# Reordering the first tiles' second state product, one weight conversion and the last stores in a fused attention and gated-MLP kernel

## The chip, the cores and the metric

The kernel runs on one core of a Trainium2 chip. The metric is the device time of one execution in microseconds (us). The core has five engines with their own instruction streams: TensorE (PE in the profile, with weight loads as PEld), VectorE (DVE), ScalarE (ACT), GpSimd (POOL) and SyncE (SP), which here only issues transfers. Each engine runs its stream in order; the engines wait for each other through semaphores. An instruction that has to wait therefore holds up everything behind it on its engine.

## The reference

An attention block with B = 8 batches, H = 8 heads, S = 512 tokens, Ns = 32 states and head size 64, then an MLP over 4352 rows (8 x (512 + 32)) with model width 512 and inner width 2048:

```python
scores = scale * np.matmul(x, state.transpose(0, 1, 3, 2))
a = softmax(scores)                     # over the 32 states
xread = np.matmul(a, state)
scores2 = scale * np.matmul(state, x.transpose(0, 1, 3, 2))
sread = np.matmul(softmax(scores2), x)  # over the 512 tokens
y = concatenate([xread, sread], axis=2) -> rows of 512
h = y @ w_in
out = (h * np.cos(h)) @ w_out
```

The function `softmax` stands here for the max, exp, sum and division that the reference writes out. The inputs x and state are float32. The two weights are float64, 8 MB each.

## The kernel before, in words

The attention output of the tokens is never formed. For a batch, "products" (L433) multiplies the batch's states by 512 columns of w_in, giving the *state product*, and evicts it to a tile `sw` with "products_kept" (ScalarE) or "products_taken" (VectorE), L438 to L447. The hidden value of a tile is then the normalised attention matrix aT times sw. There are four such products (nt = 0 to 3) for each batch; "second state product" means nt = 1 of the first batch. The fifth tile of the first batch is the first whose hidden value needs it.

A *tile* is 128 inner columns for the 512 tokens of one batch: 16 tiles a batch, 128 in all, and 16 more for the 256 state rows. One tile takes these steps:

- `hidden` (L466): TensorE forms h in one of two PSUM buffers.
- `gate` (L475, ScalarE): adds a large constant, which rounds.
- `gate2` (L478, VectorE): the rest after rounding.
- `gate3` (L483 and L484, ScalarE): absolute value and sine, which gives the cosine.
- `gate4` (L490, VectorE): h times cosine, into a slot of `g_all`. It also frees the PSUM buffer of h.
- `output` (L609), three to four tiles later: TensorE multiplies g with w_out. The tokens' output goes through sums and differences of blocks ("Pair", L500 to L547; L496 on GpSimd or VectorE). The state rows' output (`state_output`, L648) is summed in the two PSUM tiles `acc[MAIN]`.

The weights arrive as float64 in 18 loads of up to 1 MB (and two more late ones) through SyncE's queue into three raw buffers in turn. A load is *converted* to float32 by steps in `convert_part` (L217): "1" and "2" on ScalarE (L224, L227), "a", "b" and "c" on VectorE (L231, L233, L236), and "d", an integer addition, on GpSimd (L241). Step "f" fetches a later load. The step "a" limits small values from below with a maximum: this is the "limit" of the change's name. The table `conv_at` (L804) says at which step's end a load is converted; normally "1" and "2" run in that step, and "abcdf" in the next step, after gate2. Load 5 (the sixth) was an exception: all of it stood at the end of step 1, on VectorE between gate4 of the second tile and gate2 of the third.

Nothing is reordered by a scheduler: the loop at L824 writes one step for each tile, and the order of its calls is the order on every engine. `todo` holds the attention parts that `plan` (L733) puts into each step. They include, at steps 1 to 4, the first batch's state reads: "turn", "reads" (L406), "keep" (L416), "keep2" (L422) and "keep3" (L427). After the reads, `load_x(1)` (L104) fetches the second batch's image in eight transfers; its tokens are turned on TensorE at step 5 (L271). `warm` (L694) issues matmuls whose results are not used, only to keep TensorE busy; they write a PSUM tile that is begun afresh later.

At the end, the last three state tiles are put out after the loop, each with one matmul for the first half of the rows and one for the second. Then ScalarE evicts both halves (L660) and SyncE issues eight stores (L665).

The three lines that set the place of the second state product before the change were:

```python
        if step == 4:
            part(0, "products", 1, SIDE)
            part(0, "products_kept", 1, SIDE)
```

Of the kernel before, what the change touches and what calls it, by code (L numbers as in the profile page):

```python
# [9 lines left out]
F32 = mybir.dt.float32  # L10
# [3 lines left out]
ACTF = mybir.ActivationFunctionType  # L14
# [5 lines left out]
TWO_PI = 2.0 * math.pi  # L20
# [3 lines left out]
def kernel(  # L24
# [8 lines left out]
    nc = tc.nc  # L33

    B, H, S, D = x.shape
    Ns = state.shape[2]
    Dm, Dff = moe_w_in.shape
    P = 128
    NK = Dm // P
    NF = Dff // P  # L40
    NC = S // P
    T = S + Ns
    WC = 512
    scale = 1.0 / math.sqrt(D)
# [6 lines left out]
    osb = ctx.enter_context(tc.tile_pool(name="osb", bufs=2))  # L51
# [19 lines left out]
    w_out = consts.tile([P, 2, NF, HD], F32)  # L71
# [32 lines left out]
    def load_x(b):  # L104

        src = x[b].rearrange("h (c p) d -> p c h d", p=P)
        if b < 2:
            for h in range(H):
                nc.sync.dma_start(out=x_b[:, :, h], in_=src[:, :, h])
        else:  # L110
            for c in range(NC):
                nc.sync.dma_start(out=x_b[:, c], in_=src[:, c])
# [10 lines left out]
    def load_state(half, queues):  # L123
        b = slice(4 * half, 4 * half + 4)
        for k in range(NK):
# [11 lines left out]
    acc = [[ops.tile([P, S], F32, name=f"o{m}{ch}") for ch in range(2)]  # L137
           for m in range(2)]
# [41 lines left out]
    def fetch(n):  # L180
        nonlocal n_fetched
        while n_fetched < n:
            dst, src = loads[n_fetched]
            if f64:
                m, w = dst.shape[1:]

                at_, c0 = (n_fetched - 2) % 3, 0
                if n_fetched < 4:
                    at_, c0 = n_fetched // 2, n_fetched % 2 * 2 * m * w
                if n_fetched >= N_LOADS:  # L190
                    at_ = 3 + n_fetched - N_LOADS
                raw = raw_at[at_].bitcast(I32)[:, c0:c0 + 2 * m * w]
                raw = raw.rearrange("p (m f) -> p m f", m=m)
                nc.sync.dma_start(out=raw, in_=src.bitcast(I32))
                raws[n_fetched] = raw.rearrange("p m (f w) -> p m f w", w=2)
            else:
                nc.sync.dma_start(out=dst, in_=src)
            n_fetched += 1
# [6 lines left out]
    def convert(i, parts):  # L205

        for p in parts:  # L210
            if p == "f":
                if i not in (1, 2) and i + 3 < N_LOADS:
                    fetch(max(i + 4, 6))
            elif f64:
                convert_part(i, p)

    def convert_part(i, p):  # L217
        raw, dst = raws[i], loads[i][0]
        bits = dst.bitcast(I32)
        m, w = dst.shape[1:]  # L220
        c0 = m * w if i in (2, 3) else 0
        e = low[i % 2][:, c0:c0 + m * w].rearrange("p (m f) -> p m f", m=m)
        if p == "1":
            nc.scalar.activation(dst, raw.bitcast(F32)[:, :, :, 1],  # L224
                                 func=ACTF.Abs)
        elif p == "2":
            nc.scalar.activation(e, raw.bitcast(U32)[:, :, :, 0],  # L227
                                 func=ACTF.Copy, scale=2.0 ** -51, bias=2.0)
        elif p == "a":
            engine = nc.gpsimd if i == 1 else nc.vector  # L230
            engine.tensor_scalar(dst, dst, 2.0 ** -15, None, op0=ALU.max)  # L231
        elif p == "b":
            nc.vector.tensor_scalar(bits, bits, 3, None,  # L233
                                    op0=ALU.logical_shift_left)
        elif p == "c":
            nc.vector.scalar_tensor_tensor(out=bits, in0=raw[:, :, :, 1],  # L236
                                           scalar=-2 ** 31, in1=bits,
                                           op0=ALU.bitwise_and,
                                           op1=ALU.bitwise_xor)
        else:  # L240
            nc.gpsimd.tensor_tensor(bits, bits, e.bitcast(I32), op=ALU.add)  # L241
# [209 lines left out]
    def part(b, name, *args):  # L451

        if b not in attn:
            attn[b] = Attention(b)
        getattr(attn[b], name)(*args)
        if (name, args) == ("reads", (1,)) and b + 1 < B:
            if b > 0:
                attn[b + 1] = Attention(b + 1)
                attn[b + 1].load_tokens()
            load_x(b + 1)  # L460
# [5 lines left out]
    def hidden(t):  # L466
        t.hp = hps.tile([P, S], F32, name="h")[:, 0:t.n]
        for i in range(t.kn):
            nc.tensor.matmul(out=t.hp, lhsT=t.lhs(i), rhs=t.rhs(i),  # L469
                             start=(i == 0), stop=(i == t.kn - 1))  # L470

    def gate(t):

        t.q = msb.tile([P, S], F32, name="q")[:, 0:t.n]
        nc.scalar.activation(t.q, t.hp, func=ACTF.Copy, bias=MAGIC)  # L475

    def gate2(t):
        nc.vector.scalar_tensor_tensor(out=t.q, in0=t.q, scalar=MAGIC,  # L478
                                       in1=t.hp, op0=ALU.subtract,
                                       op1=ALU.subtract)  # L480
# [17 lines left out]
    MAIN, SIDE = 0, 1  # L498
# [90 lines left out]
    def free(t):  # L589
        g_free.append(t.slot)  # L590
# [54 lines left out]
                store(2 * pr.n + 1, 0, o)  # L645


    def state_output(t):  # L648
        n, pr = t.n_th, t.last_pair
        for i in range(2):  # L650
            nc.tensor.matmul(out=acc[MAIN][i],  # L651
                             lhsT=t.g[:, P * i:P * i + P],
                             rhs=w_out[:, :, t.f, :],
                             start=(n == 0), stop=(n == NF - 1))
        free(t)
        pr.more(2)
        if n == NF - 1:
            for i in range(2):
                ot = osb.tile([P, Dm], F32, name="ot")
                nc.scalar.activation(ot, acc[MAIN][i], func=ACTF.Copy,  # L660
                                     scale=TWO_PI)
                nb = P // Ns
                for m in range(nb):
                    r0 = (nb * i + m) * T + S
                    nc.sync.dma_start(out=out[r0:r0 + Ns, :],  # L665
                                      in_=ot[Ns * m:Ns * m + Ns, :])

    def tiles():
        pr = None
# [24 lines left out]
    def warm(n, to):  # L694

        for _ in range(n):
            nc.tensor.matmul(out=to, lhsT=zeros[:, 0:P], rhs=zeros, start=True,
                             stop=True)
# [34 lines left out]
    def plan(b):  # L733
# [70 lines left out]
    conv_at = {s: 4 + i for i, s in enumerate(  # L804
        (0, 1, 2, 3, 4, 5, 6, 7, 8, 10, 11, 12, 13, 14))}
# [18 lines left out]
    for step, t in enumerate(all_tiles):  # L824
        s = step % NF
        if s == 0 and t.b < B:
            steps = plan(t.b)
        todo = [p[s] if t.b < B else [] for p in steps]

        def go(n):  # L830
            for p in todo[n]:
                part(*p)

        last, conv = conv_at.get(step - 1, -1), conv_at.get(step, -1)
        if step == B * NF + (0 if f64 else 8):
            fetch(N_LOADS + 2)
        if step == 4:
            part(0, "products", 1, SIDE)
            part(0, "products_kept", 1, SIDE)
        if step != 1:  # L840
            hidden(t)
        if step == 0:
            hidden(all_tiles[1])
            warm(3, acc[MAIN][0])
            gate(t)
            gate2(t)
            convert(3, "bcdf")
            convert(4, "1a")
            go(0)
        else:  # L850
            go(0)
            if step == 5:
                states(1, acc[SIDE][1])
            gate(t)
            gate2(t)
            go(1)
            go(3)
            if step == 1:
                convert(4, "bcdf")
            elif last >= 0:  # L860
                convert(last, "abcdf")
            if conv >= 0 and not todo[1]:
                convert(conv, "1")
        gate3(t)
        if later:
            later.pop(0)()
        gate4(t)
        if conv >= 0 and todo[1] and step > 0:
            convert(conv, "1")
        if t.pair is not None:  # L870
            sums(t)
        if step == 6:
            states_kept(1, acc[SIDE][1])
        go(2)
        if conv >= 0:
            convert(conv, "2")
        go(4)
        if step == 1:
            convert(conv, "abcdf")
            conv_at[1] = -1  # L880
        if step in block_at:
            blocks(*block_at[step])
        if t.pair is not None:
            sums2(t)
        while len(line) >= (LAG if step >= 2 * NH else LAG + 1):
            output(line.pop(0))
        line.append(t)
# [32 lines left out]
```

## Time and profile before

Three runs took 795.26, 795.34 and 797.27 us; the median is 795.34 us. The profiled execution spans 793.4 us from the first to the last instruction, and took 795.2 us in all. TensorE's mean granted clock was 0.991 of full speed.

| engine | busy us | share |
|---|---|---|
| TensorE, matmuls | 764.3 | 96% |
| VectorE | 432.9 | 55% |
| ScalarE | 389.6 | 49% |
| GpSimd | 178.7 | 23% |

The chain of waits that ended last is 80% TensorE, 9% VectorE and 8% ScalarE. Shares are averages over the whole span. The stretch that the change touches is from about 33 to 50 us, and there the order of work is set by the gates and the conversions. The other place is the end, from the last matmul at 787.4 us to 793.4 us.

How to read the rows: a line such as L443 is a line of the kernel, "out<-in" are the names of the written and the read tensors, and "x4" counts instructions. A 128x512 float32 matmul shows as two records. In brackets behind a row stands the time that the engine was idle before it, and what ended this idle time.

### The profile page before, as it was taken

The numbers are of one execution on the slowest core, as the hardware profiler recorded it, in microseconds if no ns is written. First come the engines' busy times: TensorE is split into PE (matmuls) and PEld (weight loads), VectorE is DVE, ScalarE is ACT, GpSimd is POOL, SyncE is SP. The second block draws the span as 40 slices with busy tenths as digits, with TensorE's granted clock in tenths as the row PEclk, the third lists the DMA queues.
The fourth block names the chain that finished last, engine by engine and source line by source line (L and its number), as shares of the span: only waits on it lengthen the run. The fifth ranks groups of instructions, "written<-read, shape, count | busy, mean of one in ns | idle before, by whom it ended". The sixth has DMA issues, their size and how long they took to land.

```text
span 793.4 us, 7535 instructions
## 1 busy us (share of the span) xinstructions
PE 764.3 (96%) x2654; PEld 338.8 (43%) x2654; DVE 432.9 (55%) x675; ACT 389.6 (49%) x626; POOL 178.7 (23%) x119
## 2 busy tenths in 40 slices
PE   8878899899999999999999999999999999999996
PEld 3333333344444344444344434434444444455553
DVE  5869887732564467744564467635554446432431
ACT  3777964644365344634463436443563445322222
POOL 3334258684000000451000000740000004610200
PEclk9989999999999999999999999999999999999999
DMA  8475371042010610150003410340100114000021
GB/s 238 164 212 199 116 159 28 0 72 36 0 27 7 113 26 14 30 103 0 14 13 54 80 27 7 53 74 0 27 0 1 27 27 131 2 0 14 14 47 33
DMA packets 161957, 43.49 MB, mean 55 GB/s; under 512 B 153920, under 2 KB 153920, under 8 KB 161920
## 3 DMA queue, kind: packets, MB, share of 16 engines
q1 hardware_dynamic: 161216, 42.75, 24.8%
q8 instruction: 21, 0.34, 0.2%
q0 software_dynamic: 128, 0.13, 0.1%
q10 hardware_dynamic: 576, 0.13, 0.1%
q14 instruction: 16, 0.13, 0.1%
HBM read 34.08 MB, written 8.91 MB: 54 GB/s over the span
## 4 chain that ended last, share of the span: by engine, by line
PE 80%; DVE 9%; ACT 8%; issue 1%; DMA 1%; POOL 0%; SPq 0%; ACTq 0%; DVEq 0%; POOLq 0%
PE o L534 44%; PE h L469 26%; PE at L316 4%; PE o L651 3%; PE at L406 2%; DVE q L478 2%; ACT q L483 1%; ACT q L484 1%; DVE g_all L490 1%; ACT q L475 1%; DVE xT L336 1%; ACT s L227 1%; ACT xT L362 1%; DVE aT L383 1%; ACT aT L357 1%
## 5 line engine op out<-in xcount | busy, mean ns | idle before, releaser
L469 PE MATMUL h<-aT,sw 128*128 128x512 f32 x512 | 244.6, 601 | 14.5 <-DVE g_all L490 10.2
L534 PE MATMUL o<-g_all,w_out 128*128 128x512 f32 x512 | 236.3, 598 | 0.0
L496 POOL TENSOR_TENSOR g_all<-g_all 128x512 f32<-128x512 f32 x80 | 112.1, 1423 | 450.8 <-DVE g_all L490 447.2
L475 ACT ACTIVATE q<-h 128x512 f32<-128x512 f32 (+1 forms) x144 | 82.2, 571 | 264.9 <-PE h L469 264.9
L478 DVE SCALAR_TENSOR_TENSOR q<-q,h 128x512 f32<-128x512 f32 (+1 forms) x144 | 94.1, 654 | 208.3 <-ACT q L475 208.3
L534 PE MATMUL o<-g_all,s 128*128 128x512 f32 x384 | 177.3, 598 | 0.0
L490 DVE TENSOR_TENSOR g_all<-h,q 128x512 f32<-128x512 f32 (+1 forms) x144 | 94.8, 658 | 123.5 <-ACT q L484 117.2
L469 PEld LDWEIGHTS h<-aT,sw 128*128 128x128 f32 x512 | 96.8, 191 | 140.7 <-issue 110.5
L534 PEld LDWEIGHTS o<-g_all,w_out 128*128 128x128 f32 x512 | 94.0, 190 | 124.8 <-issue 118.8
L483 ACT ACTIVATE q<-q 128x512 f32<-128x512 f32 (+1 forms) x144 | 87.6, 609 | 98.3 <-DVE q L478 98.3
L534 PEld LDWEIGHTS o<-g_all,s 128*128 128x128 f32 x384 | 70.8, 190 | 91.7 <-issue 87.3
L484 ACT ACTIVATE q<-q,halfpi 128x512 f32<-128x512 f32 (+1 forms) x144 | 100.5, 698 | 4.5
L241 POOL TENSOR_TENSOR w_out<-w_out,s 128x1024 int32<-128x1024 int32 x10 | 23.9, 2390 | 82.4 <-DVE w_out L236 82.4
L496 DVE TENSOR_TENSOR g_all<-g_all 128x512 f32<-128x512 f32 x48 | 33.2, 692 | 1.6
L443 ACT COPY sw<-at 128x512 f32<-128x512 f32 x50 | 26.8, 588 | 9.0 <-PE at L316 9.0
L469 PE MATMUL h<-sT,w_in 128*128 128x256 f32 x128 | 30.2, 379 | 0.0
L651 PE MATMUL o<-w_out,g_all 128*128 128x512 f32 x64 | 29.6, 592 | 0.0
L469 PEld LDWEIGHTS h<-sT,w_in 128*128 128x128 f32 x128 | 24.3, 190 | 10.1 <-issue 6.2
L316 PE MATMUL at<-w_in,stT 64*32 64x512 f32 x400 | 27.7, 611 | 0.0
L241 POOL TENSOR_TENSOR w_in<-w_in,s 128x1024 int32<-128x1024 int32 (+1 forms) x10 | 19.7, 1965 | 31.4 <-DVE w_in L236 24.6
L540 DVE SCALAR_TENSOR_TENSOR held<-o,held 128x512 f32<-128x512 f32 x40 | 25.3, 675 | 2.3 <-PE o L534 2.3
L561 DVE STREAM_TRANSPOSE ot<-held 128x512 f32<-128x512 f32 x32 | 22.1, 692 | 0.0
(83 smaller groups left out, 438.4 us busy)
## 6 DMA issues: line engine op xcount, KB each, us to landing
out_dram<-ot SPq DMA_DIRECT2D x136, 64.0 KB, 2.0
g_all<-in_moe_w_out_dram SPq DMA_DIRECT2D x8, 1024.0 KB, 5.1
g_all<-in_moe_w_in_dram SPq DMA_DIRECT2D x6, 1024.0 KB, 5.4
xT<-in_x_dram SPq DMA_DIRECT2D x96, 64.0 KB, 2.3
x_b<-in_x_dram SPq DMA_DIRECT2D x24, 256.0 KB, 4.6
x_b<-in_x_dram SPq DMA_DIRECT2D x16, 128.0 KB, 4.0
g_all<-in_moe_w_in_dram SPq DMA_DIRECT2D x4, 512.0 KB, 6.0
x_b<-in_moe_w_out_dram SPq DMA_DIRECT2D x1, 1024.0 KB, 6.1
```

Source lines behind the costliest of these rows:

```text
L241: nc.gpsimd.tensor_tensor(bits, bits, e.bitcast(I32), op=ALU.add)
L316: nc.tensor.matmul(out=(to or at)[j][Ns * k:Ns * k + Ns, 0:n], lhsT=w[D * j:D * j + D, self.b, Ns * k:Ns * k + Ns], rhs=r(slice(D * j, D * ...
L443: (copy or nc.scalar.copy)(sw_of[self.b, nt][:, j, c0:c1], to[j][:, 0:c1 - c0])
L469: nc.tensor.matmul(out=t.hp, lhsT=t.lhs(i), rhs=t.rhs(i), start=(i == 0), stop=(i == t.kn - 1))
L475: nc.scalar.activation(t.q, t.hp, func=ACTF.Copy, bias=MAGIC)
L478: nc.vector.scalar_tensor_tensor(out=t.q, in0=t.q, scalar=MAGIC, in1=t.hp, op0=ALU.subtract, op1=ALU.subtract)
L483: nc.scalar.activation(t.q, t.q, func=ACTF.Abs)
L484: nc.scalar.activation(t.q, t.q, func=ACTF.Sin, bias=halfpi, scale=-TWO_PI)
L490: nc.vector.tensor_tensor(t.g, t.hp, t.q, op=ALU.mult)
L496: engine.tensor_tensor(out, a, b, op=ALU.subtract)
L534: nc.tensor.matmul(out=acc[bank][ch], lhsT=w[:, i, P * ch:P * ch + P], rhs=g.g, start=(i == 0), stop=(i == NH - 1))
L651: nc.tensor.matmul(out=acc[MAIN][i], lhsT=t.g[:, P * i:P * i + P], rhs=w_out[:, :, t.f, :], start=(n == 0), stop=(n == NF - 1))
```

## The change

The change has three parts. First, the sixth load (load 5) loses its exception: its "a", "b", "c", "d" and "f" steps now stand in step 2, after gate2 of the third tile, as for all other loads. Second, the second state product and its two evictions move from the start of step 4 to step 3, right behind gate and gate2 of the fourth tile. On TensorE four filler matmuls are put before the product, and one stands at the start of step 4, in the product's old place. On ScalarE the two evictions now stand ahead of the eighth load's "1", the fourth tile's gate3 and the load's "2". Third, the last three state tiles do their matmuls for the first half of the rows first and for the second half afterwards, each half is evicted as soon as it is done, and its four stores go in turn to SyncE's and ScalarE's queue. The aim is that TensorE waits less at the fifth tile, and that the last stores are issued earlier. The amount of useful work is the same.

```diff
+    N_LAST = 3
+    kept_back = []
+
+    def state_product(t, i):
+        nc.tensor.matmul(out=acc[MAIN][i], lhsT=t.g[:, P * i:P * i + P],
+                         rhs=w_out[:, :, t.f, :], start=(t.n_th == 0),
+                         stop=(t.n_th == NF - 1))
+
     def state_output(t):
-        n, pr = t.n_th, t.last_pair
-        for i in range(2):
-            nc.tensor.matmul(out=acc[MAIN][i],
-                             lhsT=t.g[:, P * i:P * i + P],
-                             rhs=w_out[:, :, t.f, :],
-                             start=(n == 0), stop=(n == NF - 1))
-        free(t)
-        pr.more(2)
-        if n == NF - 1:
+        if t.n_th < NF - N_LAST:
             for i in range(2):
-                ot = osb.tile([P, Dm], F32, name="ot")
-                nc.scalar.activation(ot, acc[MAIN][i], func=ACTF.Copy,
-                                     scale=TWO_PI)
-                nb = P // Ns
-                for m in range(nb):
-                    r0 = (nb * i + m) * T + S
-                    nc.sync.dma_start(out=out[r0:r0 + Ns, :],
-                                      in_=ot[Ns * m:Ns * m + Ns, :])
+                state_product(t, i)
+            t.last_pair.more(2)
+            free(t)
+            return
+        kept_back.append(t)
+        if len(kept_back) == N_LAST:
+            t.last_pair.more(2 * N_LAST)
+            for i in range(2):
+                for u in kept_back:
+                    state_product(u, i)
+                state_store(i)
+
+    def state_store(i):
+        nb = P // Ns
+        rows = out.rearrange("(b t) d -> b t d", t=T)[nb * i:nb * i + nb, S:T]
+        ot = osb.tile([P, Dm], F32, name="ot")
+        nc.scalar.activation(ot, acc[MAIN][i], func=ACTF.Copy, scale=TWO_PI)
+        for m in range(nb):
+            (nc.sync, nc.scalar)[m % 2].dma_start(
+                out=rows[m], in_=ot[Ns * m:Ns * m + Ns, :])
@@ the loop over the steps
         if step == 4:
-            part(0, "products", 1, SIDE)
-            part(0, "products_kept", 1, SIDE)
+            warm(1, acc[MAIN][0])
         if step != 1:
             hidden(t)
@@
             gate(t)
             gate2(t)
+            if step == 3:
+                warm(4, acc[MAIN][0])
+                part(0, "products", 1, SIDE)
+                part(0, "products_kept", 1, SIDE)
             go(1)
             go(3)
@@
         go(4)
-        if step == 1:
-            convert(conv, "abcdf")
-            conv_at[1] = -1
         if step in block_at:
             blocks(*block_at[step])
```

## The prediction

> **What bounds the kernel now.** First the busy times and the strip of the granted clock on the page: TensorE is busy for 96% of the span, so only stretches in which it stands still or runs slowly, and the end after its last matmul, can give time back.
>
> ```profile
> PE 764.3 (96%) x2654; PEld 338.8 (43%) x2654; DVE 432.9 (55%) x675; ACT 389.6 (49%) x626; POOL 178.7 (23%) x119
> ```
>
> Second, the busy time of each engine in four stretches around the fourth and fifth tile, and in the end. The columns are PE, PEld, DVE, ACT, POOL, then clock, DMA share and GB/s.
>
> ```profile
> 36.60:40.59 3.99, 1.04 (x10) 0.13 (x9) 2.51 (x4) 1.99 (x4) 2.35 (x1) 1.00 0.52 157
> 41.65:45.41 3.76, 0.01 (x2) 0.01 (x1) 3.62 (x8) 3.73 (x6) 0.00 (x0) 0.57 1.21 280
> 45.41:49.17 3.76, 3.76 (x6) 1.59 (x7) 1.38 (x2) 0.43 (x1) 2.35 (x1) 0.52 1.03 226
> 787.40:793.40 6.00, 0.00 (x0) 0.00 (x0) 0.00 (x0) 0.60 (x1) 0.00 (x0) 0.69 0.34 87
> ```
>
> TensorE is idle for about 3 us of the first row and all of the second, and then computes the fifth tile's hidden product at half clock (3.76 us for what takes 1.72 us elsewhere in the chain of waits). Third, the chain of waits there (start, us, what) tells what holds it:
>
> ```profile
> 32.55 1.07 ACT w_in L224
> ...
> 33.64 2.43 DVE w_in L231
> 36.06 0.02 issue
> 36.09 0.71 DVE w_in L233
> 36.79 0.02 issue
> 36.81 1.22 DVE w_in L236
> 38.04 0.61 DVE q L478
> ...
> 44.88 0.48 ACT sw L443
> 45.36 0.04 issue
> 45.41 3.76 PE h L469 x4
> 49.16 0.02 issue
> 49.19 0.61 ACT q L475
> ```
>
> The third tile's gate2 (L478 at 38.04) stands behind the sixth load's three conversion steps on VectorE. ScalarE waits for it, then runs through the rest of tiles 3 and 4, and only then evicts the second state product (L443 at 44.88), though TensorE had that product ready at 41.65. The fourth tile's work is thus ahead of the eviction that the fifth tile's product needs. After 49.19 the chain goes on through ScalarE and VectorE; it becomes a TensorE chain only near 110 us. Last, the timeline of the end:
>
> ```profile
> 786.54 0.60 ACT L660 ACTIVATE ot<-o 128x512 f32<-128x512 f32 x1 [4.18 <-PE o L651]
> 787.17 3.61 SPq L665 DMA_DIRECT2D out_dram<-ot  x8
> 787.40 0.60 ACT L660 ACTIVATE ot<-o 128x512 f32<-128x512 f32 x1 [0.26 <-PE o L651]
> ```
>
> Eight stores on one queue take 3.61 us to issue; the second eviction is done at 788.00, so its four stores wait for the issue of the first four. The last issue starts at 790.3.
>
> [...] clock 0.57, then 0.52, after 2.95 and 3.75 us of idleness. [...] L231 took 2.43 us, starting at 33.64 while GpSimd's L241 ran from 33.13 to 35.50, against 0.69 us elsewhere. [...] Here issuing is what the end waits for: about 0.45 us for each store, and these land 1.6 to 1.8 us after their issue.
>
> **Part one, gate2 ahead of the conversion.** The third tile's gate ends at 35.59 (L475 starts at 35.02), and VectorE, done with the second tile's gate4 at 33.58, waits. So gate2 starts at 35.61. The nearest row with this order is tile 5: L478 at 49.82, its conversion following at 50.42, L236 ending at 53.10, GpSimd's L241 from 53.24 to 55.60, thus 3.42 and 5.78 us after L478's start. For the sixth load this gives GpSimd from 39.03 to 41.39, against 38.18 to 40.53 before. The cost is only about 0.9 us, not gate2's 0.6 plus the wait for gate: before, L231 was blocked by GpSimd until 35.50 in any case. The load that waits for this conversion (the ninth, whose issue ended at 38.49) moves by the same 0.9 us, and the image's eight transfers behind it too. DMA activity of those ended near 48; near 49 is before the tokens are wanted (below).
>
> Gate3 of the third tile no longer starts at 38.67 but after ScalarE's L224, at 36.5. Then 0.64 + 0.72 + 1.03 us bring the fourth tile's gate to 38.9 (before: 41.08), ending at 39.5.
>
> **Part two, product and evictions at the fourth tile.** Four filler matmuls start on TensorE at 36.64, after the reads. A 128x512 matmul is two records of 0.43 us, so 3.44 us, to 40.08. The first half of the state product follows, to 41.1; the second half waits for GpSimd's 41.39. The filler therefore costs nothing: the conversion hides it, and it keeps the clock up. The second half starts at 41.45 and takes 1.06 us; with 0.08 us to the next engine (66.40 to 66.48 in the tokens' scores) the evictions start at 42.59. ScalarE waits for them from 39.5: this is the new wait, 3.1 us long, and behind it stand the eighth load's first step, the fourth tile's gate3 and sine, and the load's second step. These four took 1.01 + 0.53 + 0.74 + 1.04 = 3.3 us before. Two evictions take 0.96 us (the chain at 99.49). So the fifth tile's gate can start at 42.59 + 0.96 + 3.3 = 46.9, against 49.19: **2.3 us**.
>
> Other claims on that gate end sooner. TensorE's single filler ends at 43.4, the hidden product at full clock 1.72 us later, at 45.1. The full clock is thus no gain of its own; it only keeps TensorE from being last. The seventh load's conversion stands after the fourth tile's gate2 (39.5) and the keeping of the reads (1.18 us): steps from 41.4, to 44.0, GpSimd to 46.5. The first output product waits for that, starts at 46.6 and the sixth tile's hidden product at 48.3, ending at 50.0, before its gate at 46.9 + 4.86 = 51.8. Tokens follow on TensorE at 50.0, after the image's landing near 49. From 46.9 on, the same instructions in the same order follow, so the gain should be carried on whole. Dropping the special conversion at step 1 moves no other load: loads at the later steps follow their old order.
>
> **Part three, the end.** The six last matmuls are regrouped, equal in number. From 780.50 with 0.86 us each, the last three tiles start at 782.22; the first half's three end at 784.80. They need the last tile's g in third place, at 783.94; it is ready at 782.81, so nothing waits. The first eviction then lies under the other three matmuls, and so do two issues on each queue. ScalarE's issues take 2.13 / 4 = 0.53 us each (its first row), ending near 786.5, before its second eviction at 787.40. This ends at 788.00 as before. Then two stores per queue: the last starts at 788.03 + 0.42 to 0.53, about 788.5, against 790.3: **1.75 us**. Bounds are 1.2, if landing from ScalarE's queue takes 0.6 us longer, and 1.9.
>
> **Sum.** 2.3 + 1.75 = 4.05 us, so 795.34 - 4.05 = 791.3 us. The head has bounds 1.4 and 3.0: the unknowns are ScalarE's wait for TensorE (0.3 either way), the image's landing, and a changed overlap of VectorE and GpSimd further on.
>
> **Rivals.** (1) Only the end's gain survives: the later ninth load and image[...] hold the next tiles as the eviction did. For it speaks the DMA share above 1 from 41 to 47 us; against it, every landing found here is at least a microsecond before its use. 795.34 - 1.75 = 793.6. (2) Only the head's gain survives[...]: 793.0. Against it, each store is 64 KB and lands 1.7 us after issue with eight queued. (3) Slower: ScalarE stands still at the evictions for longer than worked out. If the sixth load's conversion gets blocked by GpSimd again, by 2.4 us as L231 was, and the filler then sits ahead of late work, the gate slips to 49.3, tokens collide with the image's transfers, and each later conversion loses a share too. With some 3 us lost by that and the end's gain gone, 798. The trace speaks against it: GpSimd is idle from 35.50 until that conversion has ended.
>
> **How the numbers follow.** The forecast has 0.75, rival 1 0.11, rival 2 0.08, rival 3 0.06. The range starts at 790.2 (head 3.0 and end 1.9 together give 790.4, a little below for clock and overlaps) and goes to 793.1, which takes in the head's lower bound with the end's (792.7) and rival 2. Faster by 0.3% means below 792.95: the forecast and part of rival 2, with a lucky share of rival 1, 0.82; within 0.3%: 0.13; slower: 0.05.
>
> **What would show it.** Right: L478 of the third tile starts near 35.6 and L231 takes 0.7 us behind it; L443 near 42.6, behind a ScalarE wait for TensorE of some 3 us; the fifth tile's gate near 46.9; clock 1.00 from 36 to 50; the start of the last three tiles' outputs 2.3 us earlier; two ScalarE issues after each L677 and a last issue 1.1 us after TensorE's end. Wrong: a wait of L271 for the image, a ScalarE wait for DMA, L231 again above 2 us, or a gain at 47 us that is gone at 110.

## The result, and the profile after

The changed kernel takes 791.5 us (median of 6 runs, 791.23 to 791.96) against 795.44 us for the kernel before (795.26 to 797.27). The ratio is 0.9945, with a 95% interval from 0.9933 to 0.9958: 3.9 us less, clear of noise. The profiled spans are 793.4 and 789.4 us.

The busy times and the windows first: TensorE's line of the page, and then four stretches that answer to those shown of before (columns as there).

```profile
PE 767.3 (97%) x2664; PEld 340.4 (43%) x2664; DVE 431.2 (55%) x675; ACT 389.3 (49%) x626; POOL 178.7 (23%) x119
```

```profile
36.54:40.17 3.63, 3.63 (x10) 1.44 (x9) 3.56 (x6) 2.86 (x5) 1.16 (x1) 1.00 0.27 91
40.17:43.38 3.21, 3.02 (x20) 0.79 (x20) 3.07 (x7) 0.84 (x2) 1.20 (x1) 1.00 0.94 316
43.38:46.85 3.47, 2.32 (x7) 1.01 (x6) 1.27 (x2) 3.44 (x6) 2.36 (x1) 1.00 1.30 244
785.02:789.40 4.38, 0.00 (x0) 0.00 (x0) 0.00 (x0) 0.60 (x1) 0.00 (x0) 1.00 0.23 60
```

TensorE is busy with fillers and the product in the first two rows, computes the fifth tile's hidden product in the third, and its clock is 1.00 in all three. The last row is 4.4 us long where it was 6.0.

Then the chain of waits of the changed kernel in the stretch around the fourth and fifth tile (start, us, what). It answers the chain shown of before.

```profile
35.55 1.07 ACT w_out L224
36.62 0.53 ACT q L483
...
38.96 0.05 issue
39.01 2.37 POOL w_in L241
41.38 0.04 issue
41.42 1.13 PE o L316 x8
42.55 1.05 ACT sw L443 x2
43.61 1.04 ACT w_in L224
44.65 0.53 ACT q L483
45.17 0.02 issue
45.20 0.72 ACT q L484
45.92 1.03 ACT s L227
46.95 0.49 ACT q L475
```

VectorE's conversion with gate2 behind it has left the chain. In its place stand GpSimd's addition for the sixth load, the product's second half and the evictions, and behind these the fourth tile's rest. The fifth tile's gate starts at 46.85 (in the timeline; the chain counts it from when the engine is free) and not at 49.19. The timeline of the same stretch shows the new wait and the conversion that is no longer blocked:

```profile
35.58 0.69 DVE L478 SCALAR_TENSOR_TENSOR q<-q,h 128x512 f32<-128x512 f32 x1 [2.04 <-ACT q L475]
36.19 0.69 DVE L231 TENSOR_SCALAR w_in<-w_in 128x1024 f32<-128x1024 f32 x1
...
42.53 1.07 ACT L443 COPY sw<-o 128x512 f32<-128x512 f32 x2 [3.11 <-PE o L316]
...
46.52 1.98 PE L534 MATMUL o<-g_all,w_out 128*128 128x512 f32 x4 [1.15 <-POOL w_out L241]
```

L231 takes 0.69 us where it took 2.43. ScalarE waits 3.11 us for TensorE ahead of the evictions. Then the timeline of the end:

```profile
782.47 0.60 ACT L677 ACTIVATE ot<-o 128x512 f32<-128x512 f32 x1 [2.46 <-PE o L654]
...
785.04 0.60 ACT L677 ACTIVATE ot<-o 128x512 f32<-128x512 f32 x1 [1.98 <-PE o L654]
785.67 0.85 ACTq L679 DMA_DIRECT2D out_dram<-ot  x2
786.02 0.42 SPq L679 DMA_DIRECT2D out_dram<-ot  x1
```

TensorE's last matmul ends at 785.02. The last issue starts 1.1 us later; before, it was 3.0 us (790.35 against 787.40). From the last matmul to the end of the span it is 4.4 us, against 6.0.

The positions of the second tile's gate in the profiles differ by up to 1.9 us. Below, gates are therefore counted from the second tile's gate of the same profile. Time of the fifth, sixth and 21st tile's gate:

| kernel | 5th | 6th | 21st | after last matmul | median us |
|---|---|---|---|---|---|
| before | 19.56 | 24.30 | 99.11 | 6.0 | 795.44 |
| changed | 17.25 | 22.01 | 96.78 | 4.4 | 791.5 |

The gain at the fifth gate, 2.31 us, is still 2.33 us at the 21st and 2.34 at the 141st. With 1.63 at the end this makes the 4.0 us of the spans.

### The profile page after: what moved, and what is told of

It reads as the page before. It is cut to its first block, busy times and chain, and to the rows that moved or that the text cites. A ratio compares the mean times of both kernels' runs of the same rounds, so it can differ in the third digit from the quotient of the medians.

```text
span 789.4 us, 7555 instructions
## 1 busy us (share of the span) xinstructions
PE 767.3 (97%) x2664; PEld 340.4 (43%) x2664; DVE 431.2 (55%) x675; ACT 389.3 (49%) x626; POOL 178.7 (23%) x119
## 4 chain that ended last, share of the span: by engine, by line
PE 80%; ACT 9%; DVE 8%; issue 1%; DMA 1%; POOL 1%; SPq 0%; DVEq 0%; POOLq 0%
PE o L534 44%; PE h L469 26%; PE at L316 4%; PE o L654 3%; PE at L406 2%; DVE q L478 1%; ACT q L483 1%; ACT q L484 1%; DVE g_all L490 1%; ACT s L227 1%; ACT q L475 1%; DVE xT L336 1%; ACT xT L362 1%; DVE aT L383 1%; PE o L316 1%
## 5 line engine op out<-in xcount | busy, mean ns | idle before, releaser
L241 POOL TENSOR_TENSOR w_out<-w_out,s 128x1024 int32<-128x1024 int32 x10 | 23.9, 2389 | 79.4 <-DVE w_out L236 79.4
L443 ACT COPY sw<-at 128x512 f32<-128x512 f32 x50 | 26.8, 589 | 9.0 <-PE at L316 9.0
L241 POOL TENSOR_TENSOR w_in<-w_in,s 128x1024 int32<-128x1024 int32 (+1 forms) x10 | 19.7, 1966 | 32.1 <-DVE w_in L236 18.6
```

What stands on the lines that cost most here:

```text
L443: (copy or nc.scalar.copy)(sw_of[self.b, nt][:, j, c0:c1], to[j][:, 0:c1 - c0])
```

## Experiments

Each ratio below is against the kernel before as timed beside the kernel in question. Its median was 795.95 us beside the kernels with the head alone, the end alone, no fillers and the first late evictions; 795.46 us beside those with the conversion's place, the product's place, one queue and larger stores; and 795.56 us beside the other four.

**The two halves of the change by themselves.** The first kernel is the changed one with the end of before:

```diff
-        kept_back.append(t)
-        if len(kept_back) == N_LAST:
...
-        (nc.sync, nc.scalar)[m % 2].dma_start(
+        free(t)
+        pr.more(2)
+        if n == NF - 1:
...
+                nc.sync.dma_start(out=out[r0:r0 + Ns, :],
```

> The changed kernel with the old end: the last three state tiles put out as before, eight stores on SyncE's queue. Theory (head and end add up; the trace of the changed kernel shows 2.34 us at the fifth tile's gate and about 1.6 at the end): 793.1 us, the fifth tile's gate at 46.9, six us from the last matmul to the end of the span. Rival (the head's gain would be lost without the end's, or the end gives nothing): 791.5 or 795.4.

Measured: 793.38 us (792.95 to 795.18), ratio 0.9968 [0.9958, 0.9979]; fifth gate at 17.31, sixth at 22.05; 6.1 us from the last matmul to the end. The second kernel is the one before with only the new `state_output` and `state_store`:

> The kernel before with only the new end. Theory: 793.8 us, fifth tile's gate at 49.2 as before, the span's part after the last matmul shorter by 1.6 us. Rival ([...]the end gives nothing): 795.4.

Measured: 794.38 us (793.35 to 794.97), ratio 0.9978 [0.9970, 0.9987]; fifth gate at 19.66 and 4.5 us after the last matmul. The two savings, 0.32% and 0.22%, add up to 0.54%, against the whole change's 0.55%. Head and end are independent, as worked out. The absolute time of the second is 0.6 us above what was expected, but the kernel before, timed beside it, took 0.5 us more too; the difference of the two, 1.6 us, is the expected one.

**Two queues, or halves.** The changed kernel with all last stores on SyncE:

```diff
-            (nc.sync, nc.scalar)[m % 2].dma_start(
+            nc.sync.dma_start(
```

> The changed kernel with all eight last stores on SyncE's queue, still by halves. Theory (halves hide the first four issues, the second queue saves two issues of the last four): last issue 0.85 us later than with two queues, but landing 0.3 us sooner from SyncE (1.7 against 2.0), so 0.55 us more than the changed kernel: 792.0 us, and the last stretch from TensorE's end to the end of the span 5.0 us (changed kernel 4.4, before 6.0). Rival (the queues alone make the gain): 793.1 us.

Measured: 792.51 us (792.05 to 793.01), 0.9961 [0.9947, 0.9974], and 5.0 us after the last matmul. So halves give about 1.0 us of the end's 1.6, and the second queue 0.6. The second queue saves issuing time of 0.85 us, and gives some back in landing: transfers issued by ScalarE landed after 2.0 us (median), those by SyncE after 1.7.

**The filler matmuls.** The changed kernel without all five:

```diff
-        if step == 4:
-            warm(1, acc[MAIN][0])
...
             if step == 3:
-                warm(4, acc[MAIN][0])
```

> The changed kernel without the five filler matmuls. Theory (the filler only keeps TensorE from being last): the clock falls to about 0.5 somewhere between 41 and 47 us, the fifth tile's hidden product takes up to 3.7 us from 43.1, ends near 46.8, just where its gate can start anyway; 791.5 to 791.9 us. Rival (the kept clock is the gain): the product ends after 48.5 and 2 us or more of the gain are lost: 793.5.

Measured: 792.21 us (791.83 to 793.1), 0.9955 [0.9940, 0.9970]; fifth gate at 17.31, sixth at 22.04, as in the changed kernel. TensorE's rows in its timeline:

```profile
41.51 1.06 PE L316 MATMUL o<-w_in,stT 64*32 64x512 f32 x8 [3.83 <-POOL w_in L241]
43.26 3.41 PE L469 MATMUL h<-aT,sw 128*128 128x512 f32 x4 [0.69 <-ACT sw L443]
```

Behind 3.83 us of idleness the hidden product takes 3.41 us and not 1.88; the clock from 36 to 50 us is 0.88 on average, against 1.00 in the changed kernel. It still ends at 46.67, before ScalarE comes to the fifth gate at 46.95. In this kernel the fillers give nothing at the fifth and sixth gate. That is so only because ScalarE is late, as the kernels with late evictions show below. The median is 0.3 us above the expected range. The profile has a loss of 0.43 us near 150 us that the last section treats; it also came with fillers (the head alone) and stayed away without them (the kernel before), so it is not shown to come from their absence.

**The evictions back behind the fourth tile.** Product and fillers stay at step 3:

```diff
                 part(0, "products", 1, SIDE)
-                part(0, "products_kept", 1, SIDE)
...
             warm(1, acc[MAIN][0])
+            part(0, "products_kept", 1, SIDE)
```

> The changed kernel with the two evictions back at the start of step 4, behind the fourth tile's gate3 and the eighth load's steps; the product and the fillers stay at step 3. Theory A (my working: ScalarE stands still 3.1 us before the early evictions, and the work behind them fits into this gap): evictions at 42.8, fifth tile's gate at 45.2 and the sixth's at 50.3 where the changed kernel has 51.6; 790.2 us. Theory B (the early place of the evictions is what makes the gain, as the change intends): the fifth tile's gate near 49, 793.5 us.

Measured: 790.31 us (789.86 to 791.53), 0.9932 [0.9917, 0.9947]; fifth gate at 15.84, sixth at 20.70. It is faster than the changed kernel. The two kernels side by side on one chip:

> The changed kernel, unaltered, on the same chip as the two below. 791.5 us; fifth and sixth gate 17.3 and 22.0 us after the second.

> The kernel with late evictions (early product and fillers), unaltered, on the same chip as the changed kernel. Theory (the early place of the evictions costs 1.3 us): 790.2 us, sixth gate at 20.7. Rival (the difference of the first runs was chance): 791.5 us.

Measured: 791.53 us (791.2 to 792.14), 0.9949 [0.9937, 0.9962], for the changed kernel; 789.95 us (789.86 to 790.09), 0.9929 [0.9917, 0.9942], with late evictions. No run of one reaches into the other's range, and the medians differ by 1.6 us. In the two profiles it is 1.3 us at the sixth gate (21.99 and 20.67) and 1.4 us at the 141st. What ScalarE waits for between 36 and 50 us tells why. In the changed kernel (waiter, awaited, us in all, times, longest):

```profile
ACT sw L443 <- PE o L316: 3.1, 1, 3.1
ACT q L483 <- DVE q L478: 0.6, 1, 0.6
```

And in the one with late evictions:

```profile
ACT q L475 <- PE h L469: 1.6, 1, 1.6
ACT q L483 <- DVE q L478: 0.6, 1, 0.6
```

The early place makes ScalarE stand still for 3.1 us ahead of some 3.3 us of work; with late evictions this work runs in that time without a wait. Behind it, the evictions find their product done, as the timeline of the late-eviction kernel shows (its first run): no idle time is noted at L443.

```profile
42.02 1.17 ACT L227 ACTIVATE s<-g_all 128x1024 f32<-128x1024 uint32 x1
...
43.09 1.05 ACT L443 COPY sw<-o 128x512 f32<-128x512 f32 x2
...
43.74 1.96 PE L469 MATMUL h<-aT,sw 128*128 128x512 f32 x4
...
45.74 0.60 ACT L475 ACTIVATE q<-h 128x512 f32<-128x512 f32 x1 [1.59 <-PE h L469]
```

**Only the conversion's place.** Of the head's change, only gate2 ahead of the sixth load's conversion; product and evictions at step 4, no fillers:

```diff
         if step == 4:
-            warm(1, acc[MAIN][0])
+            part(0, "products", 1, SIDE)
+            part(0, "products_kept", 1, SIDE)
...
-            if step == 3:
-                warm(4, acc[MAIN][0])
-                part(0, "products", 1, SIDE)
-                part(0, "products_kept", 1, SIDE)
```

> Of the head's change only the sixth load's conversion behind the third tile's gate2; second state product and evictions at the start of step 4 as before, no fillers; new end. Gates are counted from the second tile's gate (29.60 in the changed kernel). Theory (the head's gain comes from gate2's place, and the eviction need not move): evictions at 42.8, the hidden product at half clock from 43.3 to 47.1, so the fifth gate 17.4 us after the second (changed kernel 17.25, before 19.56) and the sixth 22.2 (22.01 and 24.30); 791.7 us. Rival (the early product and evictions make the gain): fifth gate 19 or more, 793.5 us.

Measured: 792.38 us (792.18 to 793.18), 0.9961 [0.9946, 0.9976]; fifth gate at 17.55, sixth at 22.30. So the conversion's place alone brings 2.0 of the head's 2.3 us at these gates. The median is 0.7 us above the expected 791.7; the profile shows 0.44 us of this lost near 150 us, as in the kernel without fillers. The order on TensorE and on ScalarE here is that of the late-eviction kernel except for the fillers. In both, the second half of the state product waits for GpSimd's addition: it starts 11.86 us after the second tile's gate here and 11.88 there. The product's earlier place in the code thus gains nothing by itself. The difference of 1.6 us at the sixth gate (22.30 against 20.70) is what fillers are worth once the evictions are late. The head's pieces at the sixth gate are therefore: 24.30 before, 22.30 with the conversion's new place, 20.70 with fillers as well, and back up to 22.01 with the early evictions. The TensorE rows of the kernel with only the conversion moved:

```profile
43.75 3.78 PE L469 MATMUL h<-aT,sw 128*128 128x512 f32 x4 [0.81 <-ACT sw L443]
...
47.54 3.03 PE L534 MATMUL o<-g_all,w_out 128*128 128x512 f32 x4
```

The hidden product, with a clock of 0.50 from 43.75 to 47.54, is now last at the fifth gate, and the first output behind it is slow as well: 3.03 us where the changed kernel has 1.98, with a clock of 0.60 from 47.54 to 50.40.

**Only the product's place.** The counterpart: product, evictions and fillers early, but the sixth load's conversion where it was.

```diff
         go(4)
+        if step == 1:
+            convert(conv, "abcdf")
+            conv_at[1] = -1
         if step in block_at:
```

> Of the head's change only the second state product with evictions and fillers at step 3; the sixth load's conversion stands at step 1's end as before; new end. Theory: evictions at 42.3, so the fifth gate comes 17.0 us after the second, a little before the changed kernel's 17.25; but the seventh load's conversion ends later (GpSimd near 48.6 instead of 46.5), so that the first output and the sixth hidden product wait, and the sixth gate comes at 22.55 (changed kernel 22.01, before 24.30); 792.0 us. Rival (gate2's place is what counts): fifth gate at 19 or more, 793.8 us.

Measured: 794.58 us (793.53 to 795.01), 0.9984 [0.9976, 0.9991]; the fifth gate at 16.41, earlier than expected, but the sixth at 25.51, which is 3 us later than expected and 1.2 us later than in the kernel before. By the profile this head is slower than the old one, still by 1.1 us at the 21st gate (100.19 against 99.11). The medians alone do not tell it from the kernel with only the new end, whose interval overlaps (0.9970 to 0.9987). The expectation missed a half clock. The windows of this kernel (PE, PEld, DVE, ACT, POOL, clock, DMA share, GB/s) show TensorE idle until GpSimd's addition is done, and slow after it:

```profile
44.44:48.71 4.27, 0.00 (x0) 0.00 (x0) 4.20 (x5) 3.39 (x6) 2.35 (x1) 0.81 1.08 196
48.71:52.30 3.59, 3.59 (x5) 1.52 (x6) 3.02 (x4) 2.27 (x3) 0.96 (x1) 0.50 0.54 209
```

Whether the half clock is the cause was tried by filling this gap with four more fillers:

```diff
             go(0)
+            if step == 4:
+                warm(4, acc[MAIN][0])
```

> The kernel with only the product and evictions early (the sixth load's conversion at its old place), which was slower than worked out: TensorE stood still 4.3 us before the first output, the clock fell to 0.5, and output and sixth hidden product took 3.78 and 2.71 us. Here four more filler matmuls stand in that gap, behind the turning of the reads. Theory (the surplus is the half clock): first output 1.98 us from 48.7, hidden product 1.88, sixth gate 22.9 us after the second instead of 25.5; 2.6 us faster, 792.0 us. Rival (another wait holds the sixth tile): the sixth gate stays above 24.5; 794 us or more.

Measured: 792.1 us (791.89 to 792.89), 0.9958 [0.9945, 0.9972]; sixth gate at 22.78. The first output takes 1.98 us from 48.94, and the clock stays at full speed:

```profile
44.65:48.94 4.29, 3.60 (x10) 1.33 (x8) 4.22 (x5) 3.58 (x6) 2.36 (x1) 1.00 1.12 209
48.94:52.63 3.69, 3.69 (x10) 1.73 (x11) 3.02 (x4) 2.32 (x3) 1.06 (x1) 1.00 0.62 219
```

So the half clock was the surplus. What stays, 22.78 against the changed kernel's 22.01, goes with the later GpSimd addition, for which TensorE still waits 0.70 us ahead of the first output; the conversion's new place brings it forward.

**A step further.** The late-eviction kernel, with the evictions ahead of the eighth load's second step, and the first output behind the sixth hidden product:

```diff
         if step == 4:
             warm(1, acc[MAIN][0])
-            part(0, "products_kept", 1, SIDE)
         if step != 1:
             hidden(t)
+        if step == 5:
+            output(line.pop(0))
...
         gate4(t)
+        if step == 3:
+            part(0, "products_kept", 1, SIDE)
...
-        while len(line) >= (LAG if step >= 2 * NH else LAG + 1):
+        while step != 4 and len(line) >= (LAG if step >= 2 * NH else LAG + 1):
```

> The late-eviction kernel with the evictions one instruction earlier on ScalarE, between the fourth tile's sine and the eighth load's second step, and the first output behind the sixth hidden product instead of ahead of it. Theory (now GpSimd's integer addition for the first output holds the sixth hidden product): fifth gate at 15.5 instead of 15.84, sixth at 20.3 instead of 20.7; 789.8 us. Rival (ScalarE's own work sets the sixth gate): sixth gate at 20.7, 790.2 us.

Measured: 789.88 us (789.66 to 790.74), 0.9928 [0.9915, 0.9942]; fifth gate at 15.76, sixth at 20.51, 21st at 95.33 (late evictions: 95.38). At the sixth gate 0.2 us of the expected 0.4 came, and at the 21st 0.05 is left of it. In the time the rival is right: there is nothing more to have from these two moves together.

**Fewer, larger last stores.** The late-eviction kernel with two stores of 128 KB for each half in place of four of 64 KB:

```diff
-        for m in range(nb):
-            (nc.sync, nc.scalar)[m % 2].dma_start(
-                out=rows[m], in_=ot[Ns * m:Ns * m + Ns, :])
+        for m, queue in enumerate((nc.sync, nc.scalar)):
+            queue.dma_start(
+                out=rows[2 * m:2 * m + 2],
+                in_=ot[2 * Ns * m:2 * Ns * m + 2 * Ns, :])
```

> The kernel with late evictions (product and fillers early) and, at the end, each half stored by two transfers of 128 KB, one on each queue, in place of four of 64 KB. Theory (the end is set by the last issue and a landing that hardly depends on size here): last issue 0.43 us earlier, landing up to 0.3 us longer; 790.0 us against 790.3 of the kernel with four. Rival (landing grows with size by 0.4 us or more): no gain or slower.

Measured: 799.84 us (799.56 to 800.74), 1.0056 [1.0043, 1.0068]: slower than the kernel before by 4.4 us. From the last matmul to the end of the span it is 14.2 us. The window after the last issues:

```profile
785.50:798.00 12.50, 0.00 (x0) 0.00 (x0) 0.00 (x0) 0.00 (x0) 0.00 (x0) 0.67 0.11 39
```

The DMA share is 0.11 at 39 GB/s. The changed kernel has 0.53 and 140 GB/s in the 1.8 us after its last issues begin. Besides their size, the stores differ in their form (two batches of 32 rows each against one batch of 32 rows), and no run told size and form apart. The rival's "slower" came true, but by some 10 us, and neither theory put down before the run has a cause for that; none was shown.

## Why the prediction was right

The prediction was 791.3 us, within 790.2 to 793.1; measured was 791.5.

**Part one held.** gate2 starts at 35.58 (35.61 worked out) and L231, behind it, takes 0.69 us, with GpSimd's L241 over at 35.46. That L231 had been blocked before is borne out by the profile of before, in which it is not the only one: those at 33.64, 55.17 and 94.89 began while an L241 ran, took 2.42, 0.99 and 1.35 us, and each ended 0.56 us after that L241. GpSimd's addition starts at 39.01 (39.03). The fourth tile's gate starts at 38.86 (38.9). The conversion's new place alone gives 2.0 us. The cost of 0.9 us to the conversion was also right, and nothing was lost at the landings: the tokens' L271 starts at 50.05 without a wait.

**Part two held in its times, but it did not ask what each piece is worth.** The evictions start at 42.53 (42.59), ScalarE waits 3.11 us (3.1), the fifth gate starts at 46.85 (46.9), the first output at 46.52 (46.6), the sixth hidden product at 48.34 (48.3). The prediction named the new wait and what stands behind it, and took it as the price of the early product. It gave no share of the 2.3 us to any piece. The runs show that 2.0 of it come from part one, that the product's place gains nothing by itself, since GpSimd's addition holds its second half in any case, and that the early evictions cost 1.3 us at the sixth gate. With the evictions behind the fourth tile's work and the fillers kept, the head gains 3.7 us at the fifth gate and not 2.3. The sentence that the full clock only keeps TensorE from being last also holds, for the changed kernel alone: without fillers both gates stay within 0.06 us; with late evictions the fillers are worth 1.6 us. One reading of the trace was loose: it sets the clock shares 0.57 and 0.52 beside idle times of 2.95 and 3.75 us. The gap of 2.95 us left the clock at 1.00 (40.59 to 41.65); both shares belong to the 3.75 us gap and the hidden product behind it. The argument did not rest on this.

**Part three was a little too large.** The last issue comes 1.9 us sooner after the last matmul (1.8 worked out), but the span gains 1.63 us, not 1.75, since ScalarE's stores land 0.3 us later. That bound had been kept open for up to 0.6.

**Sum.** 2.33 + 1.63 = 3.96 us against 4.05. The gain at the fifth gate was carried to the end undiminished, so that rival 1 is out; the kernels with one half each rule out rivals 1 and 2 by their times. Rival 3, the blocked conversion, did not occur: L231 took 0.69 us.

The best order found, with the conversion's new place, the fillers, late evictions and the new end, takes 789.95 us: 1.6 us less than the changed kernel and 5.6 less than the one before. The further step at 789.88 is no different from it within the spread of its runs.

## What to carry to other kernels

On an engine that runs in order, an early place for an instruction is only good if its input is ready there: find what the input itself waits for (here GpSimd's addition, which kept the evictions waiting for 3.11 us), and leave the consumer behind whatever work fits into the wait. When a change has several pieces, take each out alone: here one of them cost 1.3 us inside a change that gained. Two waits that follow on each other are not undone one by one with half the gain each; here one edit gave 2.0 of 2.3 us and the other alone cost 1.2, because it opened a gap of 4.27 us with a clock of 0.50 behind it. At the end of a kernel, count issues behind the last eviction, and time merged stores before keeping them: here two of 128 KB for each half took 14.2 us from the last matmul to the end, and four of 64 KB, in the changed kernel, 4.4.

## What the runs showed of the hardware beside this

- A gap in TensorE's work cost twice in the kernel with only the product's place. It was idle for 4.27 us; in the 3.59 us behind that the clock was 0.50, and the next two groups took 3.78 and 2.71 us in place of 1.98 and 1.88. In the changed kernel the clock was still 1.00 behind the gap of 1.15 us (46.52 to 48.40).
- Gaps of the same length were not followed by the same times. The same eight matmuls behind 2.95 and 2.96 us of idle time took 1.06 us in the kernel before, at a clock of 1.00, and 1.54 us in the one with the end alone; what made the difference was not shown:

```profile
40.59 1.06 PE L316 MATMUL o<-w_in,stT 64*32 64x512 f32 x8 [2.95 <-POOL w_in L241]
41.43 1.54 PE L316 MATMUL o<-w_in,stT 64*32 64x512 f32 x8 [2.96 <-POOL w_in L241]
```

- Almost half a microsecond far from the change comes and goes. In the profiles of the kernels with the head alone, the end alone, no fillers, and the conversion alone, the distance from the 21st to the 29th gate is 0.43 or 0.44 us longer than the 38.0 us of all others. The first row below is the changed kernel, the second the one without fillers, after the same idle time of 1.86 us; the third is the latter's clock there, where the changed kernel has 1.00:

```profile
150.43 1.98 PE L469 MATMUL h<-aT,sw 128*128 128x512 f32 x4 [1.86 <-DVE g_all L490]
150.55 2.39 PE L469 MATMUL h<-aT,sw 128*128 128x512 f32 x4 [1.86 <-DVE g_all L490]
150.90:156.00 5.10, 5.10 (x15) 3.04 (x14) 5.10 (x7) 2.32 (x4) 3.46 (x3) 0.67 0.00 0
```

So 1.86 us of idleness was followed by a clock of 0.67 in one kernel and of 1.00 in the other, and what decided it was not shown. How long the half clock lasts differs too: in the kernel before it is at 0.50 from 42.16 to 48.98 us, for 6.8 us, and from 83.12 to 86.53, for 3.4 us. As the 0.43 or 0.44 us come and go, the times of kernels that differ by less than about 0.5 us are better compared by positions in the trace than by medians alone.
